# A Fourier transform and two gated networks on one core: weights loaded straight to their final tiles, sign as a product, a PSUM bank for constants alone, another order of loads

## Chip, core and metric

One of the eight cores of a Trainium2 chip runs the kernel. The metric is the device time of one execution in microseconds (us); of several runs the median counts.

The core has a matrix engine (TensorE, PE in the profile), three engines for elementwise work (VectorE or DVE, ScalarE or ACT, GpSimd or POOL), and SyncE (SP), which here only issues transfers (DMA). Each engine runs its own instructions in program order and waits on semaphores for the others. SBUF is the working memory; PSUM, with eight banks, takes the matmuls' results.

## The reference

```python
def _attn_ref(x):                      # x: (2, 3008, 256)
    X = np.fft.fft(x, axis=1)
    X = np.fft.fft(X, axis=2)
    return X.real.astype(np.float32)

def _moe_ref(x, w_gate, w_val, w_out): # 6016 tokens, 256 -> 1536 -> 256
    gate = 1.0 / (1.0 + np.exp(-(x @ w_gate)))
    val = x @ w_val
    return (gate * val @ w_out).astype(np.float32)

def _moe2_ref(x, w_in, w_out):         # 256 -> 2048 -> 256
    h = x @ w_in
    g = h * np.cos(h)
    return (g @ w_out).astype(np.float32)
# out = _moe2_ref(_moe_ref(_attn_ref(x).reshape(6016, 256), ...), ...)
```

x is float32; the weights arrive as 64-bit floating point numbers.

## The kernel before

**Stages.** Stage A multiplies x with a 47-point transform in 16 chunks of 8 products (a product of 32-bit floats is two instructions on TensorE, so 16 a chunk); ScalarE copies each chunk from PSUM into D1 (line 376). Chunk c uses the pair of PSUM banks `b0 = 2 * (c % 4)` and the next (line 356). x comes in eight pairs of chunks through three buffers `raws` (`load_x2`), each load issued by SP when the pair three before it has been read. Stage B (`stage_b`, "b00" to "b15", 12 groups) and stage C (`stage_c`, "c00" to "c12", 6 pieces) finish the transform; each copies its results out as a high part (ScalarE) and a low part (VectorE, line 443), since the matmuls behind work in a shorter format and take high and low part separately. Stage C writes into `eo[0]` to `eo[5]`.

**First network.** `step1(s)` runs for s = 0 to 71: six pieces of the tokens, each with 12 slices of 128 hidden units. A step has two halves `ab(s, 0)` and `ab(s, 1)` of six matmuls; VectorE combines them (`even`, `tokens`, lines 532 and 540); ScalarE takes the sigmoid (line 688), GpSimd multiplies (line 544). Four steps later 12 matmuls with the output weights follow (`out1`, lines 554 to 557). Steps 0 and 1 stand between the last pieces of stage C.

**Second network.** 192 steps of 12 matmuls, `hid` and `out2`. Its weights, decoded during the first network's steps, are kept in DRAM (`ws`) and loaded into the places of the first network's weights as these are done with (`w2_load`).

**Decoding a weight.** A unit holds 512 weights per partition. There are a small row ("row"), 12 units w1 (hidden), 6 units wo1 (output) and 16 units w2. A 64-bit weight is two words, `lo` and `hi`. `dec_steps` gives its steps, `(engine, planned us, what to issue)`: ScalarE takes the magnitude of `hi` (line 134) and the carry of `lo` (line 135), VectorE clamps (line 115) and shifts (line 119), GpSimd adds the carry (line 130), and VectorE puts the sign back (line 148); once the first network's steps have begun, VectorE masks the sign (line 141) and GpSimd adds it. A w1 unit then takes a sum and a difference (lines 171 and 172). `hilo_steps` splits the result into a high part (ScalarE, line 156) and a low part (GpSimd or VectorE, line 154). `clamp` and `shift` read two constants, `cmax` and `cmask`, from PSUM bank 7, columns 510 and 511.

**Where units lie.** Before the change a unit is loaded into a decode buffer of 1536 words per partition (line 164): first the six tiles `eo`, each until stage C needs it (`ENDS`), later four pieces `stages` of D1, two of them only until step 1 (`TWO`). The split writes the final tile `wr`; W1 and WO1 are views of it, W2 and WO2 too.

**Order of the work.** The order on each engine is made when the program is built, by a planner. It keeps a clock for each engine (`clk`) and a list of units under way (`live`). `slot(t, us, ahead)` is called before each group of matmuls: it issues the copies left by the group before (`after`), and then `fill(e, until)` puts onto each engine whatever decode steps end by its clock before `until`. `regular` and `spend` book the copies themselves. For SP, `fill` starts a new unit, and so its load, when a decode buffer is free and lasts long enough (`LIFE`). `need(key)` issues the rest of a unit at once when the program comes to its use. The matmuls' order is fixed; only their waits depend on the rest.

## Time and profile before

| | |
|---|---|
| runs, median (lowest to highest) | 1028.37 us (1027.06 to 1029.26) |
| the profiled execution | 1028.72 us |
| its span, first to last instruction | 1026.6 us |
| TensorE busy (its clock granted) | 999.1 us, 97% (0.991 of full) |
| VectorE, ScalarE, GpSimd busy | 763.2, 768.1, 684.2 us |
| moved by DMA | 85.59 MB |
| stage A | 4.1 to 44.8 us |
| stages B and C to the first step | 44.8 to 81.7 us |
| first network | 81.7 to about 500 us |

In rows of the timeline the numbers are start and busy time in us, the engine, the line, the operation, what it writes and reads, and in brackets the engine's idle time just before, with the instruction that ended it. Matmuls in a run are merged into one row with a count.

### The profile page before, as it was taken

To read this page: it belongs to the slowest core of one execution; us is meant where nothing else is said; L and a number is where in the kernel's file an instruction comes from. 1 tells how busy PE (TensorE), PEld (TensorE's weight loads), DVE (VectorE), ACT (ScalarE), POOL (GpSimd) and SP (SyncE) were. 2 spreads that over 40 slices of the span, in tenths; PEclk is the share of its full clock that TensorE was granted. 3 is DMA by queue.
4 is the path that set the end of the run, shared out by engine and by line. 5 is a ranking of instruction groups with operands and counts; after the bars stand their busy time and mean duration, and the time that the engine had idled before them with its cause. 6 is when DMAs were issued, how large, how long until landed. Compare 5 with 4: busy or idle time off the path is not lost.

```text
span 1026.6 us, 13189 instructions
## 1 busy us (share of the span) xinstructions
PE 999.1 (97%) x4566; PEld 833.5 (81%) x4566; DVE 763.2 (74%) x1037; ACT 768.1 (75%) x1212; POOL 684.2 (67%) x531
## 2 busy tenths in 40 slices
PE   7998988999999999999999999999999999999998
PEld 7986777888888888888788888888888888888886
DVE  4698985788787877776577777777777777777775
ACT  4666664767666675674788888888889888898886
POOL 2475985998989878885365665756557565665653
PEclk9899998999999999999999999999999999999999
DMA  8611754586776666788500000000000000000000
GB/s 280 227 53 41 152 117 91 113 177 162 162 163 144 160 155 142 177 218 215 130 1 21 1 21 21 0 21 1 21 19 3 21 1 21 0 21 21 1 21 21
DMA packets 25363, 85.59 MB, mean 83 GB/s; under 512 B 3248, under 2 KB 6640, under 8 KB 24624
## 3 DMA queue, kind: packets, MB, share of 16 engines
q0 software_dynamic: 10368, 37.02, 19.5%
q1 hardware_dynamic: 14672, 47.59, 13.4%
q8 instruction: 36, 0.59, 0.2%
q14 instruction: 31, 0.25, 0.1%
q10 hardware_dynamic: 256, 0.14, 0.1%
HBM read 33.16 MB, written 14.56 MB: 46 GB/s over the span
## 4 chain that ended last, share of the span: by engine, by line
PE 87%; DVE 4%; DMA 3%; ACT 2%; POOL 2%; issue 1%; SPq 0%; ACTq 0%; DVEq 0%; POOLq 0%
PE ps L596 25%; PE ps L514 14%; PE ps L515 14%; PE ps L516 14%; PE ps L554 6%; PE ps L557 6%; PE ps L556 6%; PE ps L363 1%; DVE D L540 1%; DMA raw<-in_x_dram 1%; DMA gh<-D 1%; POOL D L544 1%; DMA eo<-in_w_dram 1%; DVE eo L148 1%; PE ps L457 1%
## 5 line engine op out<-in xcount | busy, mean ns | idle before, releaser
L622 POOL TENSOR_TENSOR h<-D,h 128x502 fp32r<-128x502 f32 x191 | 284.5, 1490 | 216.2 <-ACT h L621 203.9
L596 PE MATMUL ps<-h,wr 128*128 128x502 f32 x1152 | 291.9, 389 | 0.0
L514 PE MATMUL ps<-es,wr 128*128 128x502 f32 x672 | 263.1, 391 | 3.9 <-DVE D L540 3.5
L515 PE MATMUL ps<-es,wr 128*128 128x502 f32 x672 | 262.4, 390 | 0.0
L516 PE MATMUL ps<-es,wr 128*128 128x502 f32 x672 | 261.4, 389 | 0.0
L596 PEld LDWEIGHTS ps<-h,wr 128*128 128x128 f32 x1152 | 217.6, 189 | 44.6
L544 POOL TENSOR_TENSOR D<-D 128x502 f32<-128x502 f32 x144 | 184.5, 1326 | 56.0 <-ACT D L688 55.2
L607 DVE SCALAR_TENSOR_TENSOR D<-D,ps 128x502 f32<-128x502 int32 x192 | 130.1, 678 | 118.6 <-POOL h L622 107.7
L540 DVE TENSOR_TENSOR D<-D,ps 128x1004 f32<-128x1004 f32 x144 | 172.9, 1201 | 49.1 <-PE ps L516 30.3
L688 ACT ACTIVATE D<-D 128x1004 f32<-128x1004 f32 x72 | 75.2, 1044 | 125.7 <-DVE D L540 125.6
L514 PEld LDWEIGHTS ps<-es,wr 128*128 128x128 f32 x672 | 126.7, 189 | 32.2 <-DVE D L540 4.8
L608 DVE SCALAR_TENSOR_TENSOR D<-D 128x502 f32<-128x502 int32 x192 | 144.8, 754 | 6.6
L606 ACT ACTIVATE D<-ps 128x502 int32<-128x502 f32 x192 | 113.0, 589 | 48.0 <-PE ps L516 46.0
L516 PEld LDWEIGHTS ps<-es,wr 128*128 128x128 f32 x672 | 126.7, 189 | 26.4
L515 PEld LDWEIGHTS ps<-es,wr 128*128 128x128 f32 x672 | 126.9, 189 | 25.6
L614 DVE TENSOR_TENSOR D<-D,ps 128x502 f32<-128x502 f32 x192 | 128.9, 671 | 16.1 <-ACT D L613 16.1
L532 DVE SCALAR_TENSOR_TENSOR D<-eo,w,ps 128x502 f32<-128x502 f32 x144 | 101.4, 735 | 38.1 <-PE ps L516 37.7
L612 ACT ACTIVATE D<-D 128x502 f32<-128x502 f32 x192 | 119.2, 621 | 12.2 <-DVE D L608 9.8
L613 ACT ACTIVATE D<-D 128x502 f32<-128x502 f32 x192 | 120.0, 625 | 6.1
L557 PE MATMUL ps<-gh,wr 128*128 128x502 f32 x288 | 113.2, 393 | 4.2 <-POOL wr L154 4.2
L556 PE MATMUL ps<-gh,wr 128*128 128x502 f32 x288 | 113.7, 395 | 1.2 <-ACT wr L156 1.2
L621 ACT CAST h<-D 128x502 fp32r<-128x502 f32 x192 | 114.7, 597 | 0.2 <-DVE D L614 0.2
(89 smaller groups left out, 1073.2 us busy)
## 6 DMA issues: line engine op xcount, KB each, us to landing
gh<-D POOLq DMA_DIRECT2D x72, 502.0 KB, 4.8
D<-in_w_dram SPq DMA_DIRECT2D x17, 512.0 KB, 5.1
ws<-D SPq DMA_DIRECT2D x16, 512.0 KB, 3.5
wr<-ws SPq DMA_DIRECT2D x16, 512.0 KB, 4.9
out_dram<-D SPq DMA_DIRECT2D x24, 251.0 KB, 3.2
eo<-in_w_dram SPq DMA_DIRECT2D x11, 512.0 KB, 6.2
raw<-in_x_dram SPq DMA_DIRECT2D x15, 256.0 KB, 4.7
D<-in_wo_dram SPq DMA_DIRECT2D x6, 512.0 KB, 4.2
```

The source lines that it names most:

```text
L514: PE.matmul(o, w_hi, m_hi, start=first, stop=False)
L515: PE.matmul(o, w_lo, m_hi, start=False, stop=False)
L516: PE.matmul(o, w_hi, m_lo, start=False, stop=last)
L540: V.tensor_tensor(out=gv[s][:, :, c:c + PC], in0=sas, in1=ps[:, 6:8, 0:PC], op=op)
L544: G.tensor_tensor(out=gv[p][:, 1, m], in0=gv[p][:, 1, m], in1=gv[p][:, 0, m], op=ALU.mult)
L556: PE.matmul(o, WO1[:, f, 0, m], h[:, 0, sl], start=(f == 0), stop=False)
L557: PE.matmul(o, WO1[:, f, 1, m], h[:, 0, sl], start=False, stop=False)
L596: PE.matmul(o, WO2[:, f, i, d * 128:(d + 1) * 128], h[:, m], start=(f == 0 and i == m == 0), stop=(f == NF2 - 1 and m == 1))
L607: V.scalar_tensor_tensor(out=r, in0=k, scalar=-C1, in1=h, op0=ALU.mult, op1=ALU.add)
L608: V.scalar_tensor_tensor(out=r, in0=k, scalar=-C2, in1=r, op0=ALU.mult, op1=ALU.add)
L614: V.tensor_tensor(out=r, in0=r, in1=ps[:, 4 + s % 4, 0:PC], op=ALU.mult)
L622: (V if s == N2S - 1 else G).tensor_tensor(out=h[:, 1], in0=r, in1=f32(h[:, 0]), op=ALU.subtract)
```

## The change

The first network's weights (w1 and wo1) are loaded into tiles of the size of a final weight tile (`slot_tile`, one tag for each place); the decode reads the raw words there, works in a decode buffer, and the split writes a new tile in the same place. Loads and decoding are thus planned apart: `load_next` issues the next of the 18 loads whenever SP's clock has room, and `begin` starts a unit's decode when its load is due and a buffer is free. W1, WO1, W2 and WO2 become functions that return a view of a slot. `stages` has two pieces in place of four, and the time limit TWO goes.

Units begun after group "b05" (`masked`) take the sign from ScalarE (Sign into one word of the pair, the magnitude into the other) and a product over each pair on VectorE. The other units put the sign back before GpSimd's add; the form with a masked sign and a second add on GpSimd goes.

Stage A rotates over three pairs of banks (0 to 5), the constants stay in bank 7, the warm-up products (seven for five) write bank 6. In the first loads x's second pair goes ahead of all weights, one weight stands between the second and the third pair, and up to chunk 2 SP plans less far ahead. Both memsets of x buffers are on GpSimd. Planned times of the groups change (1.71 to 1.79, 2.54 to 2.72), as do `ENDS` and `LIFE`.

The diff, cut to its core:

```diff
-NWARM = 5
+NWARM = 7
...
-    wr = cpool.tile([128, NF1 * 8 * 128 + NF1 * 2 * 256], F32R, name="wr")
...
+    slots, gen = {}, {}
+
+    def slot_tile(u, dtype):
+
+        gen[u] = gen.get(u, -1) + 1
+        slots[u] = cpool.tile([128, 2 * UC], dtype, tag=f"u{u}", name=f"u{u}_{gen[u]}", bufs=1)
+        return slots[u]
+
+    for u in range(NF1 + NF1 // 2):
+        slot_tile(u, F32)
+
+    def W1(f):
+        return slots[f].rearrange("p (g e h m) -> p g e h m", g=2, e=2, h=2)
...
-    stages = [flat1[:, i * 3 * UC:(i + 1) * 3 * UC] for i in range(4)]
+    stages = [flat1[:, i * 3 * UC:(i + 1) * 3 * UC] for i in range(2)]
...
-    czero = ps[:, 7, 509:510].bitcast(U32)
...
+        if masked[0]:
+            mag = r[:, :, 1]
+            return [
+                (A, .52, lambda: carry(t)),
+                (A, .52, lambda: A.activation(out=r[:, :, 0], in_=hi, func=AF.Sign)),
+                (A, .52, lambda: A.activation(out=mag, in_=hi, func=AF.Abs, scale=2.0 ** -80)),
+                (V, .6, lambda: clamp(mag)),
+                (V, .6, lambda: shift(mag.bitcast(U32))),
+                (G, 1.5, lambda: add(mag, t)),
+                (V, 1.05, lambda: V.tensor_reduce(out=t, in_=r, axis=mybir.AxisListType.X, op=ALU.mult)),
+            ]
+        low = buf[:, 0:n] if direct else lo
...
-        ] + ([
-            (V, .6, lambda: V.scalar_tensor_tensor(out=hi.bitcast(U32), in0=hi.bitcast(U32), scalar=0x80000000,
-                                                   in1=czero.to_broadcast(list(hi.shape)),
-                                                   op0=ALU.bitwise_and, op1=ALU.bitwise_or)),
-            (G, 1.23, lambda: added(lo)),
-            (G, 1.23, lambda: added(hi)),
-        ] if begun[0] else [
-            (G, 1.23, lambda: added(lo)),
             (V, .6, lambda: V.scalar_tensor_tensor(out=u, in0=hi.bitcast(U32), scalar=0x80000000, in1=u,
                                                    op0=ALU.bitwise_and, op1=ALU.bitwise_or)),
-        ])
...
+            (G, 1.23, lambda: add(t, low)),
+        ]
...
+    def load(kind, i, raw):
+        DQ.dma_start(out=raw.bitcast(U32), in_=sources[kind](i).bitcast(U32))
...
-        steps = [(DQ, 1.5 * n / UC, lambda: DQ.dma_start(out=buf[:, 0:2 * n].bitcast(U32), in_=src.bitcast(U32)))]
-        steps += dec_steps(buf, n)
+        if kind in DIRECT:
+            steps = dec_steps(buf, n, slots[home(kind, i)], True)
+        else:
+            raw = buf[:, 0:2 * n]
+            steps = [(DQ, 1.5 * n / UC, lambda: load(kind, i, raw))] + dec_steps(buf, n, raw, False)
...
+    DIRECT = ("w1", "wo1")
+    queued = [("w1", f) for f in range(NF1)] + [("wo1", u) for u in range(6)]
+    todo = [("row", 0)] + queued + [("w2", u) for u in range(16)]
+    loaded = {}
...
+    def load_next():
+        k = queued.pop(0)
+        load(*k, slots[home(*k)])
+        loaded[k] = spend(DQ, 1.5) + 2.3
...
+    def begin(until):
+
+        while todo and todo[0] in loaded:
+            for bf in free:
+                at = max(loaded[todo[0]], bf[2])
+                if at <= until and at + LIFE <= bf[1]:
+                    start(bf)
+                    break
+            else:
+                return
...
         while True:
+            begin(until)
...
+                if step[0] is VG and e is V and begun[0]:
+                    continue
...
+                if e is DQ and clk[e] + 1.5 <= until:
+                    if queued:
+                        load_next()
+                        continue
+                    if len(todo) > held[0] and todo[0][0] == "w2":
...
-    LIFE, ALWAYS = 16.0, 1e9
+    LIFE, ALWAYS = 14.0, 1e9
...
-    ENDS = (44, 52, 54, 62, 70, 70)
+    ENDS = (45.5, 52.5, 57, 65, 73, 73)
...
-        G.memset(raws[1], 0.0)
-        V.memset(raws[2], 0.0)
+        for r in raws[1:]:
+            G.memset(r, 0.0)
...
         for p in range(1, NX2):
-            fill(DQ, clk[DQ] + 2.0)
             load_x2(p)
+            if p == 1:
+                fill(DQ, clk[DQ] + 1.6)
...
-            PE.matmul(ps[:, 7, 0:128], warm, warm, start=True, stop=True)
+            PE.matmul(ps[:, 6, 0:128], warm, warm, start=True, stop=True)
...
-            slot(now, 1.71, AHA if c < NJC - 2 else (4, .4, 2, .5) if c < NJC - 1 else (4, .1, 2, -.8))
-            b0 = 2 * (c % 4)
+            slot(now, 1.79, (.3,) + AHA[1:] if c < 3 else AHA if c < NJC - 2 else (4, .4, 2, .5) if c < NJC - 1 else (4, .1, 2, -.8))
+            b0 = 2 * (c % 3)
...
         if st == "b05":
-            two_end[0] = now + 6 * 1.71 + 3 * 2.54 + 2.0
-            free += [[bf, ALWAYS, now] for bf in stages[:2]] + [[bf, TWO, now] for bf in stages[2:]]
+            masked[0] = True
+            free += [[bf, ALWAYS, now] for bf in stages]
...
     def w2_load(u):
-        nc.sync.dma_start(out=f32(wr[:, u * 2 * UC:(u + 1) * 2 * UC]), in_=ws[u])
+        nc.sync.dma_start(out=f32(slot_tile(u, F32R)), in_=ws[u])
```

## Rows read from the trace of the kernel before

**Rows 1.** Busy time by stage: stretch, length, engines, granted clock, DMA share, GB/s.

```profile
0.00:4.10 4.10, 2.26 (x10) 2.29 (x11) 2.48 (x6) 0.00 (x0) 2.15 (x6) 1.00 0.53 156
4.10:44.76 40.66, 34.94 (x261) 34.34 (x260) 20.37 (x37) 22.43 (x37) 10.71 (x10) 0.87 0.85 274
44.76:81.71 36.95, 33.33 (x241) 30.64 (x241) 35.15 (x63) 24.75 (x60) 27.25 (x22) 1.00 0.21 70
106.92:147.86 40.94, 40.94 (x181) 33.91 (x180) 34.96 (x40) 26.05 (x31) 36.37 (x32) 1.00 0.62 130
190.13:500.00 309.87, 308.17 (x1350) 254.29 (x1349) 237.51 (x267) 202.94 (x235) 257.44 (x225) 1.00 0.74 173
```

**Rows 2.** Timeline of TensorE in stage A.

```profile
5.30 3.06 PE L363 MATMUL ps<-hd,raw 128*128 128x96 f32 x26
11.20 7.20 PE L363 MATMUL ps<-hd,raw 128*128 128x96 f32 x48 [2.83 <-DMA raw<-in_x_dram]
...
21.27 2.89 PE L363 MATMUL ps<-hd,raw 128*128 128x96 f32 x24 [0.65 <-DMA raw<-in_x_dram]
26.41 18.35 PE L363 MATMUL ps<-hd,raw 128*128 128x96 f32 x136 [2.25 <-DVE eo L119]
```

**Rows 3.** Timeline of VectorE before TensorE's wait of 2.25 us ends.

```profile
25.67 0.69 DVE L119 SCALAR_TENSOR_TENSOR eo<-eo,ps 128x512 uint32<-128x512 uint32 x1
```

**Rows 4.** Single microseconds after the two gaps; the clock is the third number from the end.

```profile
13.00:14.00 1.00, 1.00 (x7) 1.00 (x6) 0.68 (x2) 1.00 (x4) 0.00 (x0) 0.50 0.68 209
...
29.00:30.00 1.00, 1.00 (x7) 1.00 (x7) 0.18 (x1) 0.79 (x2) 0.00 (x0) 0.50 0.79 123
```

**Rows 5.** Timeline of ScalarE: copies of stage A's chunks out of PSUM.

```profile
10.18 0.78 ACT L376 COPY D<-ps 128x768 f32<-128x768 f32 x1
...
13.29 0.79 ACT L376 COPY D<-ps 128x768 f32<-128x768 f32 x1
...
37.65 0.80 ACT L376 COPY D<-ps 128x768 f32<-128x768 f32 x1 [0.99 <-PE ps L363]
39.44 0.80 ACT L376 COPY D<-ps 128x768 f32<-128x768 f32 x1 [0.99 <-PE ps L363]
```

**Rows 6.** Timeline of TensorE at steps 12 to 16 of the first network.

```profile
147.86 0.40 PE L514 MATMUL ps<-es,wr 128*128 128x502 f32 x1
...
154.19 0.50 PE L557 MATMUL ps<-gh,wr 128*128 128x502 f32 x1 [2.36 <-POOL wr L154]
...
179.05 0.40 PE L514 MATMUL ps<-es,wr 128*128 128x502 f32 x1
```

**Rows 7.** Timeline of SP's DMA issues between 110 and 140 us.

```profile
122.12 1.46 SPq L164 DMA_DIRECT2D D<-in_wo_dram  x2
```

**Rows 8.** Busy time by stretch at the start; the last two numbers are DMA.

```profile
0.00:5.00 5.00, 3.16 (x15) 3.19 (x16) 2.88 (x7) 0.55 (x1) 2.15 (x6) 1.00 0.61 174
5.00:25.00 20.00, 15.69 (x121) 15.26 (x120) 8.40 (x20) 11.64 (x21) 2.81 (x3) 0.91 0.95 307
```

**Rows 9.** Timelines of ScalarE and TensorE where the first network begins.

```profile
87.17 0.67 ACT L134 ACTIVATE D<-D 128x512 f32<-128x512 f32 x1 [3.00 <-DMA D<-in_wo_dram]
...
91.28 0.49 PE L457 MATMUL ps<-D2h,T3h 128*128 128x502 f32 x1 [1.26 <-ACT eo L468]
```

**Rows 10.** Groups by line and shape: count, busy us and mean ns, idle before.

```profile
L540 DVE TENSOR_TENSOR D<-D,ps 128x1004 f32<-128x1004 f32 x144 | 172.9, 1201 | 49.1 <-PE ps L516 30.3 <-ACT gh L629 13.7 <-DMA gh<-D 1.0
...
L141 DVE SCALAR_TENSOR_TENSOR D<-D,ps 128x512 uint32<-128x512 uint32 x19 | 12.9, 681 | 0.0
L148 DVE SCALAR_TENSOR_TENSOR eo<-eo 128x512 uint32<-128x512 uint32 x11 | 11.4, 1038 | 4.8 <-POOL eo L130 4.8
...
L134 ACT ACTIVATE D<-D 128x512 f32<-128x512 f32 x23 | 15.4, 670 | 4.4 <-DMA D<-in_wo_dram 3.0 <-DMA D<-in_w_dram 1.4
```

**Rows 11.** Groups by line: ScalarE's table loads, first and last of three.

```profile
L134 ACT ACT_TABLE_LOAD x1 | 1.3, 1283 | 4.5 <-DVE raw L332 4.5
...
L613 ACT ACT_TABLE_LOAD x1 | 1.3, 1283 | 0.0
```

More of the change, by code (lines that the diff above doesn't have):

```diff
@@ L120, in shift, with dec_steps, carry, add @@
                                op0=ALU.logical_shift_left, op1=ALU.bitwise_and)
-    def dec_steps(buf, n):
+    def dec_steps(buf, n, raw, direct):
+        lo, hi = (raw.rearrange("p (n t) -> p n t", t=2)[:, :, k] for k in range(2))
         r = buf[:, 0:2 * n].rearrange("p (n t) -> p n t", t=2)
-        lo, hi = r[:, :, 0], r[:, :, 1]
         t = buf[:, 2 * n:3 * n]
         u = t.bitcast(U32)
-        def added(w):
-            G.tensor_tensor(out=t.bitcast(I32), in0=t.bitcast(I32), in1=w.bitcast(I32), op=ALU.add)
+        def carry(dst):
+            A.activation(out=dst.bitcast(I32), in_=lo.bitcast(U32), func=AF.Copy, scale=2.0 ** -29)
+        def add(dst, other):
+            G.tensor_tensor(out=dst.bitcast(I32), in0=dst.bitcast(I32), in1=other.bitcast(I32), op=ALU.add)
+        if masked[0]:
[10 more added lines that the diff above has]
+        low = buf[:, 0:n] if direct else lo
@@ new lines, in hilo_steps, with high, low @@
+    def hilo_steps(views, src):
+        at = []
+        def high():
+            at[:] = views()
+            A.copy(at[0], src)
+        def low(e):
+            e.tensor_tensor(out=at[1], in0=src, in1=f32(at[0]), op=ALU.subtract)
+        return [(A, .52, high), (VG, .6, low)]
+    ws = [dpool.tile([128, 2 * UC], F32, name=f"ws{u}") for u in range(NF2)]
+    sources = {"row": lambda i: w1s, "w1": lambda i: w1[i], "wo1": lambda i: wo1[i], "w2": lambda i: w2[i]}
+    def load(kind, i, raw):
+        DQ.dma_start(out=raw.bitcast(U32), in_=sources[kind](i).bitcast(U32))
@@ L195, in cost @@
     def cost(step, e):
-        return step[1] * (2.05 if step[0] is VG and e is G else 1) + (beside[0] if e is V else 0)
+        return step[1] * ((2.5 if begun[0] else 2.05) if step[0] is VG and e is G else 1) + (beside[0] if e is V else 0)
     def step_of(un, e=None):
@@ L290, in fft_moe_moe @@
     free += [[b_, e_, 0.0] for b_, e_ in zip(flat, ENDS)]
+    start(free[0])
     after = []
@@ L445, in stage_b @@
         after.append(evac)
-        return now + 1.71
+        return now + 1.79
     def stage_c(b, ch, ahead=AHB):
-        slot(now, 2.54, ahead)
+        slot(now, 2.72, ahead)
         t = b * NCH + ch
@@ L582, in hid @@
         for k in range(2):
-            three(o, W2[:, f, k, 0], W2[:, f, k, 1], y[:, 0, k], y[:, 1, k], first=(k == 0), last=(k == 1))
+            three(o, W2(f)[:, k, 0], W2(f)[:, k, 1], y[:, 0, k], y[:, 1, k], first=(k == 0), last=(k == 1))
     def out2(s):
@@ L681, in step1 @@
         if main:
-            for un in [un for un in live if un[1] and un[1][1] < (TWO if s < 2 else ALWAYS)]:
-                finish(un)
-            free[:] = [bf for bf in free if bf[1] == ALWAYS or bf[1] == TWO and s == 0]
+            free[:] = [bf for bf in free if bf[1] == ALWAYS]
             tokens(s)
```

103 lines of the change are left out of this document (48 added, 55 removed).

## Prediction

> **What bounds the kernel now.** The profiled execution took 1028.72 us, of which the span is 1026.6; it stands 0.35 us above the median of the three runs (1028.37). I read four views, coarse to fine. First the table by stage [rows 1]: from 190.13 to 500 TensorE is busy 308.17 of 309.87 us, and of the second network behind it the change touches only the tiles that hold its weights, so nothing is for sale there. Before that, stage A (to 44.76) has idle time and a mean granted clock of 0.87. So the question is only what happens before 190 us.
>
> Second, TensorE's own timeline in stage A, the 16 chunks of the first transform [rows 2]. Its idle pieces are 2.83 us (waiting for x), 0.65 (for x) and 2.25 (for a VectorE instruction that only decodes a weight). The 2.25 is odd until one counts: the run of 24 instructions before it is chunk 6 (16) and the first half of chunk 7 (8), so the instruction that waits is the first to write bank 7 of PSUM. The constants that `clamp` and `shift` read lie in that bank at columns 510 and 511, and the matmuls write columns 0 to 383 of it: the wait is on the bank, not on data. It ends when the `shift` that starts at 25.67 is done [rows 3]. After both long gaps the granted clock is half, 1.2 in place of 2.4 GHz [rows 4]. At full clock a chunk takes 1.79 us (copies of successive chunks at 37.65 and 39.44 [rows 5]), 0.1117 us an instruction. The 136 instructions after the bank wait took 18.35 us and would take 15.2; the 48 after the x wait took 7.20 and would take 5.4. Stage A thus loses 5.7 us idle and 5.0 us to the clock; TensorE alone would end it at 4.1 + 16 x 1.79 + 0.6 (the extra products of chunk 4) = 33.3.
>
> Third, the 36.95 us from 44.76 to 81.71, stages B and C up to the first network [rows 1]: VectorE is busy 35.15 us of it, TensorE 33.33. VectorE is the co-bound here, on decoding.
>
> Fourth, the steps of the first network. From 106.92 on TensorE is busy 40.94 of 40.94 us [rows 1], at 5.46 us a step (24 matmuls). Steps 12 and 16 start at 147.86 and 179.05 [rows 6]: 31.19 us for four steps that should take 21.84. The 9.35 us are two like waits for an output unit, the first of which ends at 154.19, and their low clock. Their cause is a load: the last two output units were requested only at 122.12 [rows 7], because a unit could be loaded only into a free decode buffer.
>
> **The change part by part.**
>
> *Own bank for the constants.* Stage A now rotates over three pairs of banks, 0 to 5, and the warm-up writes bank 6. The 2.25 us wait goes and with it the 3.15 us of low clock behind it. What comes late next is data.
>
> *Order of x and weights.* I followed the planner's clock for the load queue by hand (1.5 a weight, 2.1 a pair of chunks). Old: w0, x1, w1, x2, w2, x3, w3, x4, x5, w4, x6, tables, x7. New: x1, w0, x2, w1, x3, w2, w3, x4, w4, x5, w5, x6, tables, x7, then the other 12 units in a row. So x1 no longer queues behind 512 KB, which at 307 GB/s [rows 8] is 1.7 us; of the 2.83 us I leave 1. But in front of x7 there is now one weight more. x is 96 rows of 16 x 1024 numbers, 6.3 MB; with six weights, the tables and the head it is 10.1 MB. The first 5 us moved 0.87 MB and the next 20 ran at 307 GB/s with the DMA engines 0.95 busy [rows 8], so x7 lands near 5 + 9.2/0.307 = 35, and two chunks later stage A ends near 39, by transfers, not by TensorE. On SP each x load still waits for its buffer, and behind it wait only weights that are early. **Stage A: -5.8** (bounds: -11.5, TensorE alone; 0, the low-clock stretches come back).
>
> *Loads straight into the final tiles.* All 18 loads are issued by about 35 us and need no decode buffer; no byte moves that did not move before. The decode itself is the same until stage B's sixth group. The four staging buffers in D1 become two: a raw unit no longer sits in one while it loads. The 9.35 us at steps 12 to 16 go if those units are decoded by then; with their data there 80 us earlier, they are. **-9.3** (bounds -9.4 and 0). The load that ScalarE waits 3.00 us for at 87.17 also goes, and with it the 1.26 us that TensorE then waits for ScalarE's copy [rows 9]: **-1.3** (0 to -3).
>
> *What VectorE pays.* It was busy only 20.37 of 40.66 us in stage A [rows 1] because weights were late, and what it did not do then it does in B and C. New, by 39 us the six early units are decoded: six times some 3.1 (two at 0.68, a sign instruction at 1.04 [rows 10], half of the two sums), with its other work about 27 us. Up to 81.71 it did 58.0 in all (2.48 + 20.37 + 35.15 [rows 1]). If the four output units that it decoded after that come before it, at some 2.5 each, and the memset of 1.8 goes to POOL, it is 67, so 40 are left when stage A ends and the first step starts 40 us later; if they stay behind, 30 are left and TensorE's own 12 x 1.79 + 4 x 2.73 = 32.4 decide. The planner puts them ahead wherever its clock has room, and it charges 0.6 for instructions that take 0.68 to 1.04. I take 38.5 for these stages in place of 36.95: **+1.5** (bounds -4.5, +5.5).
>
> *Sign as a product.* Units begun after stage B's sixth group take ScalarE one instruction more (0.67), VectorE two at 0.68 and a reduction over 1024 numbers in place of three at 0.68 [rows 10], and POOL one add less. No row shows the reduction; the nearest is the addition over 1004, 1.20, which I take (bounds 0.68, the 512-element form, and 2.4, twice the addition). Some 20 units pay it, 16 of them second-network weights during the steps, at +0.5 us of VectorE each. In the steps VectorE is busy 237.51 of 309.87 us [rows 1], so 1.3 of each 5.46 are free beside today's decoding, and there is one unit in 3.6 steps: **0** (if that cover were gone, 16 x 0.5 = +8; POOL's relief cannot gain while TensorE is full). Two rows stand beside each other here: the instruction with two SBUF inputs, L148, takes 1038 ns, and the like one with an input from PSUM, L141, 681 [rows 10]. The Trainium skill, page SBUF — State Buffer, section "Who interferes with whom", says that a VectorE instruction with two SBUF inputs contends with GpSimd and that a reduction on this chip never does. The trace agrees on the first half; no run here shows the second, and by it the 1.20 would hold beside a busy POOL.
>
> *Edits at nothing.* The warm-up starts 0.9 us earlier, as it no longer waits for memsets in its bank, and is two products longer; the first real matmul still comes at 4.1. The planner's new lengths (1.71 to 1.79 and so on) only change order.
>
> Sum: 1028.7 - 5.8 + 1.5 - 1.3 - 9.3 = 1013.8; against the median, **1013.5 us**.
>
> **Rivals.**
> 1. *VectorE takes all of stage A's gain.* The first step starts no earlier than now. For it: 35.15 of 36.95 us busy. Against: its idle half of stage A is now filled. 1028.4 - 1.3 - 9.3 = 1017.8.
> 2. *TensorE alone bounds B and C*, and stage A ends at 36 with 0.9 to the next matmul as now: first step at 69.3, 12.4 earlier, 1005.
> 3. *The change does not do what it says at the steps:* the last output units are loaded early but decoded late, since only two decode buffers remain, and the stalls stay. For it: the decode of those units now takes from 122 to 154 us. 1013.5 + 9.3 = 1022.8.
> 4. *Slower: the copy out of PSUM becomes the wait.* ScalarE runs in order, and a chunk's copy stands behind the first decode instruction of a weight still in flight: the copies of chunks 0 and 1 came at 10.18 and 13.29 [rows 5], 3.7 and 4.9 us after their matmuls (done by 6.5 and 8.4 [rows 2]). With four pairs a copy may be 3 x 1.79 us late, with three 2 x 1.79 = 3.6: it decides from there. If each of six early weights makes TensorE wait 2.5 us and lose 2.5 to the clock (the means of the two cases above), stage A loses 30 us and ends at 63: 1013.5 + 24 = 1037.
> 5. *Sign needs another activation table.* Now there are three table loads of 1.28 us in the whole run, the first before Abs and the last before Sin [rows 11], and Abs and copies stand between sigmoids without one. Two more for each of 16 units would be 41 us of ScalarE; with half of it hidden in its idle third, 1013.5 + 20 = 1034. The Trainium skill, ScalarE: Activation LUTs, section "Table sets: the hidden batching unit", names relu, copy, identity and abs as being in every set, and not sign; by the 2.7 us that it gives for a switch, an estimate, the 41 would be 86. The trace agrees for Abs and copy and shows no Sign.
>
> **How the numbers follow.** Forecast 0.57 (its own range 1007 to 1020), rival 1 0.15, rival 2 0.10, rival 3 0.09, rival 4 0.05, rival 5 0.04. The range takes in 1 and 2 and leaves out 3 to 5: **1005 to 1021**. A difference of 0.2% (2 us) is about what a measurement of this kernel can tell from none. Faster: forecast and rivals 1 to 3, 0.91. Slower: rivals 4 and 5 but for a mild form of them, 0.07; within 0.2%: 0.02.
>
> **What would show it.** Right: no TensorE wait on a decode instruction in stage A, and its end at 38 to 40 us; the gap at 8 to 11 us down to about 1 and no half clock behind it; the first step at 76 to 80 us; steps from the fourth on at 5.46 us with no wait for output weights; still three table loads; the reduction at 1.2. Wrong: TensorE waiting for ScalarE's copies in stage A (rival 4), TensorE waiting for VectorE's low parts in B and C (rival 1), waits for output weights after step 8 (rival 3), table loads at each unit (rival 5).

## The result, and the profile after

The changed kernel took 1012.95 us (median of four runs, 1012.53 to 1017.06) beside 1028.82 us for the kernel before on the same chip: ratio 0.985, 95% interval 0.982 to 0.989. A second set of six runs gave 1015.03 beside 1026.85: 0.989 (0.987 to 0.992). So 12 to 16 us are gone. The forecast was 1013.5.

The profiled execution of the changed kernel has a span of 1011.5 us where that of before had 1026.6. Its table by stage answers [rows 1]; columns are a stretch in us, its length, busy time (instructions) of each engine, granted clock, share of the DMA engines and GB/s:

```profile
4.10:39.79 35.69, 32.40 (x262) 31.51 (x260) 18.74 (x33) 23.15 (x39) 17.30 (x18) 0.95 1.00 337
39.79:75.16 35.37, 33.33 (x240) 30.65 (x241) 29.92 (x56) 26.07 (x63) 32.61 (x30) 1.00 0.28 109
75.16:100.79 25.63, 20.56 (x87) 15.51 (x86) 20.94 (x25) 19.13 (x29) 14.82 (x13) 1.00 0.11 21
100.79:147.31 46.52, 46.52 (x205) 38.40 (x204) 40.62 (x45) 30.89 (x38) 40.80 (x36) 1.00 0.61 125
```

Stage A ends at 39.79 instead of 44.76, the first step starts at 75.16 instead of 81.71, and from the first output product in step 4 (100.79) TensorE is busy without a gap to 147.31, where before it waited at steps 12 and 14. In stages B and C VectorE is no longer full (29.92 of 35.37 us; before 35.15 of 36.95); GpSimd is now the busier of the two.

TensorE's timeline of stage A, which answers [rows 2]:

```profile
5.25 3.33 PE L427 MATMUL ps<-hd,raw 128*128 128x96 f32 x26
9.13 5.92 PE L427 MATMUL ps<-hd,raw 128*128 128x96 f32 x48 [0.56 <-issue]
...
17.59 14.37 PE L427 MATMUL ps<-hd,raw 128*128 128x96 f32 x112 [2.08 <-ACT D L440]
32.43 7.36 PE L427 MATMUL ps<-hd,raw 128*128 128x96 f32 x64 [0.48 <-DMA raw<-in_x_dram]
```

No wait on a decode instruction is left, and the 2.83 us wait for x is gone. In their place stands one wait of 2.08 us for ScalarE's copy out of PSUM, with low clock behind it (112 instructions take 14.37 us; at 0.1117 each they take 12.5). ScalarE's timeline tells why:

```profile
12.19 0.77 ACT L440 COPY D<-ps 128x768 f32<-128x768 f32 x1
16.18 0.66 ACT L161 ACTIVATE eo<-u 128x512 f32<-128x512 f32 x1 [3.22 <-DMA u<-in_w_dram]
16.75 0.78 ACT L440 COPY D<-ps 128x768 f32<-128x768 f32 x1
```

The copy that TensorE needs stands in ScalarE's queue behind the first decode instruction of a weight that was still in flight. That is rival 4 in a mild form. The seventh pair of x chunks, whose load ends the wait at 32.43, decides when the last four chunks begin.

At the start of the network one wait stayed, which answers [rows 9]:

```profile
85.21 0.49 PE L521 MATMUL ps<-D2h,T3h 128*128 128x502 f32 x1 [1.12 <-ACT eo L532]
```

The product that replaced the masked sign, and two of the three table loads; columns: line, engine, operation, count, then busy us and mean ns of one, then idle us before it:

```profile
L156 DVE TENSOR_REDUCE D<-D 128x512 f32<-128x1024 f32 x21 | 25.4, 1212 | 0.0
L750 ACT ACT_TABLE_LOAD x1 | 1.3, 1283 | 0.0
L677 ACT ACT_TABLE_LOAD x1 | 1.3, 1283 | 0.0
```

### The profile page after: what moved, and what is told of

The parts are those of the page before. It is cut to its first block, busy times and chain, and to the rows that moved or that the text cites. A ratio compares the mean times of both kernels' runs of the same rounds, so it can differ in the third digit from the quotient of the medians.

```text
span 1011.5 us, 13127 instructions
## 1 busy us (share of the span) xinstructions
PE 993.6 (98%) x4570; PEld 828.7 (82%) x4570; DVE 764.0 (76%) x1023; ACT 782.4 (77%) x1234; POOL 670.5 (66%) x525
## 4 chain that ended last, share of the span: by engine, by line
PE 85%; POOL 4%; DVE 3%; ACT 3%; DMA 3%; issue 1%; ACTq 0%; SPq 0%; DVEq 0%; POOLq 0%
PE ps L660 26%; PE ps L578 14%; PE ps L579 14%; PE ps L580 14%; PE ps L618 6%; PE ps L620 6%; PE ps L621 6%; DVE D L604 2%; POOL eo L145 1%; DMA u<-in_w_dram 1%; DMA gh<-D 1%; POOL u L179 1%; POOL eo L206 1%; ACT gh L693 1%; ACT gh L692 1%
## 5 line engine op out<-in xcount | busy, mean ns | idle before, releaser
L660 PE MATMUL ps<-h,u 128*128 128x502 f32 x1152 | 291.8, 389 | 0.0
L578 PE MATMUL ps<-es,u 128*128 128x502 f32 x672 | 262.9, 391 | 4.9 <-DVE D L604 3.5
L579 PE MATMUL ps<-es,u 128*128 128x502 f32 x672 | 262.2, 390 | 0.0
L580 PE MATMUL ps<-es,u 128*128 128x502 f32 x672 | 261.2, 389 | 0.0
L660 PEld LDWEIGHTS ps<-h,u 128*128 128x128 f32 x1152 | 217.4, 189 | 44.7
L578 PEld LDWEIGHTS ps<-es,u 128*128 128x128 f32 x672 | 126.4, 188 | 33.6 <-DVE D L604 4.7
L580 PEld LDWEIGHTS ps<-es,u 128*128 128x128 f32 x672 | 126.5, 188 | 26.5
L579 PEld LDWEIGHTS ps<-es,u 128*128 128x128 f32 x672 | 126.6, 188 | 25.6
L620 PE MATMUL ps<-gh,u 128*128 128x502 f32 x288 | 112.5, 391 | 0.0
L621 PE MATMUL ps<-gh,u 128*128 128x502 f32 x288 | 111.8, 388 | 0.0
```

Source lines behind the costliest of these rows:

```text
L578: PE.matmul(o, w_hi, m_hi, start=first, stop=False)
L579: PE.matmul(o, w_lo, m_hi, start=False, stop=False)
L580: PE.matmul(o, w_hi, m_lo, start=False, stop=last)
L620: PE.matmul(o, WO1(f)[:, 0, m], h[:, 0, sl], start=(f == 0), stop=False)
L621: PE.matmul(o, WO1(f)[:, 1, m], h[:, 0, sl], start=False, stop=False)
L660: PE.matmul(o, WO2(f)[:, i, d * 128:(d + 1) * 128], h[:, m], start=(f == 0 and i == m == 0), stop=(f == NF2 - 1 and m == 1))
```

## The experiments

Each kernel was profiled once, and all times in this table are read from TensorE's timeline: the end of the last matmul on x (end of stage A), the first matmul of the first network, the first output matmul (step 4), the time from there to the end (rest), and the span. `before_need1` has the program of before up to step 4, and the kernels marked * have that of the changed kernel in stage A.

| kernel | A ends | to first step | to step 4 | rest | span | DMA 5 to 35 us |
|---|---|---|---|---|---|---|
| before | 44.76 | 36.95 | 25.2 | 919.7 | 1026.6 | 264 GB/s |
| before_need1 | 43.27 | 37.51 | 25.0 | 912.0 | 1017.8 | 276 |
| before_bank | 41.04 | 35.87 | 25.5 | 919.8 | 1022.2 | 304 |
| before_two | 39.78 | 36.47 | 25.2 | 912.4 | 1013.9 | 315 |
| after * | 39.79 | 35.37 | 25.6 | 910.7 | 1011.5 | 326 |
| after_again * | 42.25 | 34.68 | 25.4 | 910.9 | 1013.3 | 320 |
| after_late_wo * | 44.19 | 34.75 | 25.4 | 911.0 | 1015.3 | 306 |
| after_sigmoid_later * | 40.35 | 34.86 | 25.6 | 910.6 | 1011.5 | 320 |
| after_no_eo * | 40.65 | 34.75 | 25.3 | 913.9 | 1014.6 | 312 |
| after_two_early * | 42.89 | 34.73 | 24.5 | 922.6 | 1024.7 | 310 |
| after_sign_old | 41.74 | 36.89 | 24.6 | 910.6 | 1013.9 | 306 |
| after_copyfirst | 41.95 | 36.35 | 25.1 | 911.1 | 1014.5 | 326 |
| after_bank4 | 48.95 | 34.39 | 25.6 | 910.5 | 1019.5 | 263 |
| after_x_sooner | 40.71 | 36.52 | 27.2 | 943.8 | 1048.3 | 289 |

### The bank alone

```diff
-            b0 = 2 * (c % 4)
+            b0 = 2 * (c % 3)
...
-            PE.matmul(ps[:, 7, 0:128], warm, warm, start=True, stop=True)
+            PE.matmul(ps[:, 6, 0:128], warm, warm, start=True, stop=True)
...
```

The lines left out move the extra products of chunk 4 to that chunk's own banks, as in the changed kernel.

> The kernel before with the bank edit alone: the chunks of stage A rotate over three pairs of PSUM banks and the warm-up writes bank 6; loads, order and decoding stay as they were. Own-bank theory: the 2.25 us wait and the 3.15 us of low clock behind it go, so stage A ends at 44.76 - 5.4 = 39.4 instead of 44.76, and the waits for output weights at steps 12 and 16 stay (9.35 us). Rival, transfers: the same x chunks come no sooner and stage A still ends after 43. For the stages behind it: if VectorE (35.15 us busy of 36.95) takes the gain back, the first step still starts at 81 to 82 and the total is 1028; if it does not, the first step starts at 76.3 and the total is 1023.

Measured: 0.9966 of before (0.9949 to 0.9983), 1023.45 us beside 1026.04. TensorE's timeline of stage A in this kernel:

```profile
11.33 7.20 PE L363 MATMUL ps<-hd,raw 128*128 128x96 f32 x48 [2.98 <-DMA raw<-in_x_dram]
...
21.07 10.93 PE L363 MATMUL ps<-hd,raw 128*128 128x96 f32 x96 [0.31 <-ACT half L386]
33.68 7.36 PE L363 MATMUL ps<-hd,raw 128*128 128x96 f32 x64 [1.68 <-DMA raw<-in_x_dram]
```

The wait on the decode instruction is gone, the long run behind it goes at full clock (96 in 10.93 us), and a wait for x of 1.68 us appears late in the stage: transfers take back part of the 5.4. Stage A ends at 41.04. The first step follows at 76.91, 4.8 us earlier than in the profile of before (3.9 earlier than in before_need1, which is the same program up to there), so VectorE does not take the gain. That was rival 1, and it is out for the stages as they were before, too. Of what the profile shows, 2.6 us are left in the median of the runs.

### The bank undone in the changed kernel

```diff
-            b0 = 2 * (c % 3)
+            b0 = 2 * (c % 4)
```

> The changed kernel with four pairs of PSUM banks in stage A again, so that the constants share bank 7 with every fourth chunk; everything else as changed. Own-bank theory: TensorE waits again for a decode instruction of VectorE (line 127 or 131) before a write of bank 7, 1 to 3 us at one or two chunks, with low clock behind it: stage A ends at 41 to 45 instead of 39.79. Rival, copy order: the third pair is what costs, because the copy of chunk 2 is late by more than two chunks and less than three; then the 2.08 us wait for ScalarE's copy goes, with its 1.9 us of low clock, and stage A ends at 36 to 38.

Measured: 1020.31 us, 0.9941 of before. Stage A:

```profile
17.68 5.43 PE L427 MATMUL ps<-hd,raw 128*128 128x96 f32 x24 [5.70 <-DVE eo L127]
23.66 11.78 PE L427 MATMUL ps<-hd,raw 128*128 128x96 f32 x104
```

Two waits on VectorE's decode instructions come back, 5.70 us here and 2.20 us (for line 131) at 37.64, and stage A ends at 48.95, 9.2 us later than in the first profile of the changed kernel, 7.3 later than the mean of six (below) and 4.2 later than before. The wait on the bank is shown from both sides, and in the new order of loads it would have cost more than in the old one: 5.3 us beside 1015.03 in the median of the runs, where the bank alone gave 2.6.

### Copies ahead of weights in flight

```diff
-        loaded[k] = spend(DQ, 1.5) + 2.3
+        loaded[k] = spend(DQ, 1.5) + (6.3 if k[0] == 'w1' and k[1] < 4 else 2.3)
```

> The changed kernel, in which the planner expects the first four weights 4 us later than it does now, so that ScalarE's first decode instruction of a weight in flight stands behind two copies out of PSUM instead of ahead of them. The load queue's order is the same. Copy-order theory: the 2.08 us wait of TensorE for a copy goes, and the 1.9 us that the 112 instructions behind it lost to the clock: stage A ends at 36 instead of 39.79, and the total falls by 2 to 4 us unless decoding takes it back in the next two stages. Rival, transfers bound stage A (as predicted, near 39): the wait only moves to x, stage A ends at 39 to 40, the total moves by less than 0.5 us.

Measured: 1014.7 us, 0.9882 of before (0.9851 to 0.9913), no different from the changed kernel. Stage A:

```profile
18.82 3.78 PE L427 MATMUL ps<-hd,raw 128*128 128x96 f32 x32 [1.75 <-DMA raw<-in_x_dram]
23.48 7.55 PE L427 MATMUL ps<-hd,raw 128*128 128x96 f32 x64 [0.88 <-DMA raw<-in_x_dram]
32.97 8.98 PE L427 MATMUL ps<-hd,raw 128*128 128x96 f32 x64 [1.94 <-DMA raw<-in_x_dram]
```

The wait for the copy is gone, and x takes its place three times. So the 2.08 us of the changed kernel lay under the wait for x. The load that ends the last of these waits was issued at 22.63, 2.2 us sooner than in the changed kernel (24.84), since its buffer was free sooner, and was there no sooner (32.97 beside 32.43): that speaks for the transfers and against the three buffers of x as what holds the stage.

### The last output units loaded late

```diff
-                    if queued:
+                    if len(queued) > (0 if released[0] else 2):
...
+        if s == 8:
+            released[0] = True
+            for u in (16, 17):
+                A.copy(slots[u][:, 0:1], halfpi)
```

The line that defines `released` is left out.

> The changed kernel, in which the last two output units' loads wait for a tiny ScalarE copy into their tiles at step 8 (about 120 us), when in the kernel before they were requested too; their tiles, the direct load and all other edits stay. Load theory (the early load is what removed the stalls): ScalarE begins to decode the first of them at 128 or later instead of 123.3, TensorE waits for its weights at step 12 and perhaps at step 16 with low clock behind each, and the total rises by 5 to 9 us. Rival, decode order: the units are decoded one after the other in two buffers anyway, the load at 120 us is early enough, and the total stays within 1 us of 1013.

Measured: 1014.76 us, 0.9884 of before (0.9854 to 0.9915). ScalarE's and, in the second fence, GpSimd's timeline:

```profile
124.36 0.27 ACT L714 COPY u<-halfpi 128x1 f32<-128x1 f32 x2
...
128.63 0.67 ACT L142 ACTIVATE D<-u 128x512 int32<-128x512 uint32 x1 [2.13 <-DMA u<-in_wo_dram]
```

```profile
145.25 1.79 POOL L179 TENSOR_TENSOR u<-D,u 128x512 fp32r<-128x512 f32 x1
```

The loads were let go only at 124.5, relative to the first step even later than before (45.6 us after it; before 122.12 - 81.71 = 40.4 [rows 7]). Decoding began at 128.63, as the load theory says. But no wait for output weights came back: the rest took 911.0 us as in the changed kernel. The unit for step 12 was ready at 147.0, and that step's first output matmuls start at 149.08: two microseconds to spare. A late load, as before had it, is not enough to make the stalls.

### Decoding placed one step earlier in the kernel before

```diff
-            need(("wo1", (s - L1) // 2))
+            need(("wo1", min(5, (s + 1 - L1) // 2)))
```

> The kernel before with one edit: the decoding of an output unit has to be issued one step earlier than the step that uses it (the planner's forced finish looks one step ahead). Loads, buffers, banks and the sign's form stay as before, and the last two output units are still requested at about 122 us. Placement theory (the stalls at steps 12 and 16 came from where the planner put the decoding, not from the load): both waits go or shrink under 0.5 us and the total falls by 7 to 9 us, to about 1018. Load theory, as predicted: the data is late, the 2.36 us waits stay, and the total stays within 2 us of before.

Measured: 1018.6 us, 0.9924 of before (0.990 to 0.9947): 8.2 us less from one line that moves no load. The rest fell from 919.7 to 912.0. SP's timeline from 110 to 140 us and, in the second fence, the one wait for output weights that TensorE's timeline still shows:

```profile
120.99 1.46 SPq L164 DMA_DIRECT2D D<-in_wo_dram  x2
```

```profile
129.72 0.49 PE L557 MATMUL ps<-gh,wr 128*128 128x502 f32 x1 [1.70 <-DVE wr L154]
```

The last two units are requested 40.2 us after the first step, where before it was 40.4 [rows 7], and the pairs of waits at steps 12 and 14 are gone. This refutes the sentence of the prediction "Their cause is a load". The wait of 1.70 us is more than the 0.5 expected: the forced finish put a low part on VectorE, and that instruction took 4.88 us (from 124.78), while GpSimd was busy.

### One output unit's place undone in the changed kernel

```diff
-    ENDS = (45.5, 52.5, 57, 65, 73, 73)
+    ENDS = (45.5, 52.5, 57, 65, 66, 66)
```

> The changed kernel with one constant changed: the last two output tiles close as decode buffers at 66 instead of 73 on the planner's clock, so that two output units instead of three are decoded before the first steps of the network. All 18 loads stay where they are, done by about 45 us, straight into the final tiles. Placement theory: the third unit slips behind steps 1 to 4, in which the planner has no room on VectorE, every later unit slips with it, and TensorE waits for output weights again at step 12 or 14, 1 to 4 us a time with low clock behind it: the total rises by 5 to 10 us, to 1019 to 1025. Load theory, as predicted: with the data in place 80 us early the units are in time, and the total stays within 1.5 us of 1014.

Measured: 1024.39 us, 0.9985 of before (0.9974 to 0.9996): nearly all of the change is lost. TensorE's timeline at steps 8 and 12:

```profile
124.68 0.49 PE L620 MATMUL ps<-gh,u 128*128 128x502 f32 x1 [0.58 <-ACT u L176]
126.98 0.50 PE L621 MATMUL ps<-gh,u 128*128 128x502 f32 x1 [1.80 <-POOL u L179]
151.01 0.50 PE L620 MATMUL ps<-gh,u 128*128 128x502 f32 x1 [0.57 <-ACT u L176]
153.32 0.49 PE L621 MATMUL ps<-gh,u 128*128 128x502 f32 x1 [1.81 <-POOL u L179]
```

These are pairs like those of before at steps 12 and 14, of which [rows 6] shows one wait, though all 18 loads were issued by 42.2 us. GpSimd's timeline shows where the six units became ready. In this kernel:

```profile
77.74 1.30 POOL L179 TENSOR_TENSOR u<-D,u 128x512 fp32r<-128x512 f32 x1 [3.13 <-ACT u L176]
...
109.14 1.84 POOL L179 TENSOR_TENSOR u<-D,u 128x512 fp32r<-128x512 f32 x1
...
125.40 1.53 POOL L179 TENSOR_TENSOR u<-D,u 128x512 fp32r<-128x512 f32 x1
134.60 1.60 POOL L179 TENSOR_TENSOR u<-D,u 128x512 fp32r<-128x512 f32 x1
151.73 1.54 POOL L179 TENSOR_TENSOR u<-D,u 128x512 fp32r<-128x512 f32 x1
160.33 1.59 POOL L179 TENSOR_TENSOR u<-D,u 128x512 fp32r<-128x512 f32 x1
```

and in the changed kernel:

```profile
75.75 1.29 POOL L179 TENSOR_TENSOR u<-D,u 128x512 fp32r<-128x512 f32 x1 [0.63 <-ACT u L176]
78.88 1.30 POOL L179 TENSOR_TENSOR u<-D,u 128x512 fp32r<-128x512 f32 x1 [1.83 <-ACT u L176]
...
84.76 1.28 POOL L179 TENSOR_TENSOR u<-eo,u 128x512 fp32r<-128x512 f32 x1 [3.31 <-ACT u L176]
...
118.85 1.57 POOL L179 TENSOR_TENSOR u<-D,u 128x512 fp32r<-128x512 f32 x1
...
124.21 1.57 POOL L179 TENSOR_TENSOR u<-D,u 128x512 fp32r<-128x512 f32 x1
...
140.60 1.58 POOL L179 TENSOR_TENSOR u<-D,u 128x512 fp32r<-128x512 f32 x1
```

The changed kernel finishes three output units before the network runs at full pace; this one finishes one and has the second at 109 (I had expected two). Before had two, ready at 84.6 and 94.6. From 84.0 to 103.5 in the changed kernel (89.4 to 109.5 before), which is steps 1 to 4, VectorE decodes nothing, so in this planner's order each unit that misses the start pushes the later ones behind it, and each needs several steps of leftover time. The unit for step 12 comes at 125.8 in the changed kernel, at 153.3 here, and came at 154.1 before [rows 6].

### Two small edits to the kernel before

```diff
-            need(("wo1", (s - L1) // 2))
+            need(("wo1", min(5, (s + 1 - L1) // 2)))
...
-            b0 = 2 * (c % 4)
+            b0 = 2 * (c % 3)
```

> The kernel before with two small edits together: the own bank for the constants (three pairs of banks, warm-up in bank 6) and the decoding of an output unit issued one step earlier. Loads still go through decode buffers in their old order, the sign has its old form. Theory after the runs so far: the bank gave 0.0034 and the placement 0.0076 of the time of before, and nothing else of the change carries time; so these two edits give 0.989 of before, some 1015.4 us, as the changed kernel (0.985 to 0.989). Rival: direct loads and their order carry a part of their own in stage A and B (as predicted, about 3 us): these two edits stop at 1018 or more.

Measured: 1016.53 us, 0.9909 of before (0.9891 to 0.9926). The intervals of the changed kernel are 0.9823 to 0.9886 and 0.9871 to 0.9915, of which only the second meets it. So two small edits carry most of the change, 10.4 of its 11.8 to 15.9 us; the changed kernel's two medians lie 1.5 and 3.6 us lower still, and that may belong to the rest of the change. Part of it is visible: the forced placement leaves one wait at a step,

```profile
125.42 0.50 PE L557 MATMUL ps<-gh,wr 128*128 128x502 f32 x1 [1.72 <-DVE wr L154]
```

and the rest takes 912.4 us here, 910.7 in the changed kernel. VectorE's timeline shows the instruction that TensorE waits for and, in the second fence, a like instruction in the kernel before, where GpSimd was idle beside it:

```profile
120.47 4.90 DVE L154 TENSOR_TENSOR wr<-D,wr 128x512 fp32r<-128x512 f32 x1
```

```profile
29.82 0.69 DVE L154 TENSOR_TENSOR wr<-eo,wr 128x512 fp32r<-128x512 f32 x1 [3.46 <-ACT wr L156]
```

### The old form of the sign

```diff
-                (A, .52, lambda: A.activation(out=r[:, :, 0], in_=hi, func=AF.Sign)),
...
+                (V, .6, lambda: V.scalar_tensor_tensor(out=hi.bitcast(U32), in0=hi.bitcast(U32), scalar=0x80000000,
...
-                (V, 1.05, lambda: V.tensor_reduce(out=t, in_=r, axis=mybir.AxisListType.X, op=ALU.mult)),
+                (G, 1.23, lambda: add(t, hi)),
...
```

> The changed kernel with the old form of the sign for the units that use the product: VectorE masks the sign bits, POOL makes two additions, no Sign on ScalarE and no reduction. Prediction: worth 0, so the total moves by less than 1 us. A rival that came out of the late loads: the stalls at steps 12 and 16 went because the decoding of an output unit became shorter or was placed earlier, not because of its load; if it is the sign's form that did it, TensorE waits 1 to 3 us for the last two output units' low parts again, and the total rises by 5 to 9 us.

Measured: 1015.11 us beside 1015.03 for the changed kernel on the same chip (0.9881 and 0.9893 of before): 0, as predicted, and no stall came back. The windows from 147.31 to 500, the old form in the first fence and the changed kernel in the second (PE, PEld, DVE, ACT, POOL):

```profile
147.31:500.00 352.69, 350.71 (x1539) 289.76 (x1538) 267.83 (x303) 232.18 (x275) 282.18 (x246) 1.00 0.68 160
```

```profile
147.31:500.00 352.69, 350.83 (x1537) 289.35 (x1536) 275.46 (x304) 244.51 (x293) 261.02 (x228) 1.00 0.69 159
```

VectorE pays 7.6 us more for the product and GpSimd 21 less; TensorE is full either way. In the one profile of the old form stages B and C took 36.89 us, 2 more than in the changed kernel, with VectorE busy 34.93 of them, and the way to step 4 was 0.9 shorter; the medians of the runs show nothing of it.

### The changed kernel once more

> The changed kernel itself once more, as the control for the others on the same chip. In the look at the late output loads, stage A, whose instructions were the same, ended at 44.2 instead of 39.79, with the DMA engines moving 306 GB/s from 5 to 35 us instead of 326. If stage A is bound by transfers (as predicted), its end follows that rate from run to run: some 39.8 at 326 GB/s and 44 at 306; at a like rate the span is 1011 to 1012. If the copy order decides, it ends at 39 to 40 whatever the rate.

Measured: 1015.03 us, as above; in the profile stage A ended at 42.25 with 320 GB/s, span 1013.3. TensorE's timeline from the first copy wait on:

```profile
17.33 14.37 PE L427 MATMUL ps<-hd,raw 128*128 128x96 f32 x112 [1.54 <-ACT D L440]
33.26 8.98 PE L427 MATMUL ps<-hd,raw 128*128 128x96 f32 x64 [1.56 <-DMA raw<-in_x_dram]
```

The rate is only part of it: after_sigmoid_later ended at 40.35 with the same 320. Over six profiles of the same instructions (the kernels marked *) the end of stage A ran from 39.79 to 44.19, mean 41.7. Profiles that differ by 2 us in stage A thus tell nothing, and the 39.79 of the first one was the best of six.

### The first sigmoid behind the copies, and no weight in the output tiles

These two go together. First:

```diff
+        if s == 1:
+            A.activation(out=gv[0][:, 0], in_=gv[0][:, 0], func=AF.Sigmoid)
...
-            A.activation(out=gv[s][:, 0], in_=gv[s][:, 0], func=AF.Sigmoid)
+            if s:
+                A.activation(out=gv[s][:, 0], in_=gv[s][:, 0], func=AF.Sigmoid)
```

> The changed kernel with the first sigmoid put behind the copies of the second batch's second slice (line 532) on ScalarE, not ahead of them. Theory: TensorE's 1.12 us wait at 85.2 is for copies that stand behind that sigmoid, which itself waits for the tokens; it goes, and the total falls by 1 to 1.5 us unless the gate of step 0 now comes late. Rival: the gate of step 0 is what the next steps need, and POOL's products start later by as much: the total stays or rises by up to 1 us.

Measured: 1014.03 us (0.9885 of before), and the wait stands as it was, 1.13 us at 85.26. The theory is wrong as stated; ScalarE's timeline shows another instruction ahead of the copies:

```profile
84.11 0.62 ACT L176 CAST u<-eo 128x512 fp32r<-128x512 f32 x1 [4.11 <-DVE eo L156]
84.64 1.05 ACT L532 COPY eo<-ps 128x502 f32<-128x502 f32 x2
```

A weight was being decoded in the very tile that the copy writes, so its last instructions had to go first. The second attempt took that weight out of the tile:

```diff
-    ENDS = (45.5, 52.5, 57, 65, 73, 73)
+    ENDS = (45.5, 52.5, 57, 65, 66, 66)
...
-            need(("wo1", (s - L1) // 2))
+            need(("wo1", min(5, (s + 1 - L1) // 2)))
```

> The changed kernel in which no weight is decoded any more in the last two output tiles shortly before they are written (their closing times in the planner go from 73 to 66), and the decoding of an output unit is issued one step earlier to keep its margin. Theory: TensorE's 1.12 us wait at 85.2 is for copies (line 532) that stand behind the last instruction of a weight decoded in their target tile, which itself waits for a reduction of VectorE behind the tokens of step 0; the wait goes and the total falls by about 1 us. Rival: the unit that has to move then comes late at the steps, TensorE waits 1 to 3 us there, and the total rises.

Measured: 1015.86 us (0.9906 of before). The wait stays, 1.59 us at 85.16, and now it is the sigmoid that is ahead:

```profile
83.60 1.04 ACT L750 ACTIVATE D<-D 128x1004 f32<-128x1004 f32 x1 [2.21 <-DVE D L604]
84.55 1.52 ACT L532 COPY eo<-ps 128x502 f32<-128x502 f32 x3
```

Both were in front, and taking one away uncovered the other. Both edits together were not tried.

This kernel also bears on the output units. It differs from after_two_early in the `need` line alone, and like it has one output unit ready before the network runs at full pace (77.7 us, the second at 109.6). Its rest is 913.9 us, where after_two_early has 922.6 (medians of the runs 1015.86 and 1024.39), and none of the pairs of waits is left.

### Fewer weights ahead of x

```diff
-            slot(now, 1.79, (.3,) + AHA[1:] if c < 3 else AHA if c < NJC - 2 else
+            slot(now, 1.79, (.3,) + AHA[1:] if c < 3 else (2 if c < 5 else -9,) + AHA[1:] if c < 10 else AHA if c < NJC - 2 else
```

(with the edit of after_copyfirst)

> The changed kernel with two weights fewer (1 MB) ahead of the last two pairs of x chunks on the load queue, and with the first four weights expected 4 us later so that ScalarE's copies go first. Transfer theory: at 320 GB/s the last pair lands 3.3 us sooner and stage A ends at 37 to 39 instead of 39.8 to 42.2; the weights come later by as much, and if the decoding in the next two stages takes all of that back, the first step still starts at 75 to 77; if not, at 72 to 74 and the total falls by 2 to 3 us. Rival: copies out of PSUM or buffers of x decide, stage A stays at 40 or more.

Measured: 1049.02 us, 1.0222 of before (1.0202 to 1.0241). Stage A ended at 40.71, not at the 37 to 39 of the transfer theory but inside the spread of the six profiles, so it decides nothing between theory and rival. The loss is at the steps:

```profile
120.11 0.79 PE L620 MATMUL ps<-gh,u 128*128 128x502 f32 x1 [4.46 <-ACT u L176]
121.47 0.79 PE L621 MATMUL ps<-gh,u 128*128 128x502 f32 x1 [0.56 <-POOL u L179]
134.62 0.49 PE L620 MATMUL ps<-gh,u 128*128 128x502 f32 x1 [0.57 <-ACT u L176]
136.93 0.50 PE L621 MATMUL ps<-gh,u 128*128 128x502 f32 x1 [1.82 <-POOL u L179]
```

Such pairs stand at five steps, down to 187.97, and the rest took 943.8 us. The fifth and sixth weights were issued from 30.99 us on, where the changed kernel issues them at 14.75 and 22.10. The decoding of the output units slid behind the start of the network, and 33 us were lost, with every load issued by 44 us. The edit of after_copyfirst alone lost nothing (rest 911.1).

## Why the prediction was right, and where it was not

The time was right (1013.5 for 1012.95 and 1015.03), but in part by luck: of the four terms of the sum the one for stage A was more than twice too large, the largest had the right size for a wrong reason, and the two small ones had the wrong sign.

**Own bank for the constants: right.** The wait is on the bank, shown by doing it alone and by undoing it. Of the 5.4 us that the prediction counted for the wait and its low clock, 2.2 to 5.0 came in stage A (before 44.76 and 43.27; with the bank 41.04 and 39.78) and 2.6 in the time of the runs.

**Order of x and weights, and stage A as a whole: mis-sized.** The term was -5.8, to 39. Two profiles of the old program give 44.0, six of the new one 41.7: -2.3. Before with the bank alone ended at 41.04, with bank and placement, which has the same stage A, at 39.78. So the new order of the loads shows no gain of its own. That x comes last, by its transfers, was right: x waits took the place of the copy wait when that was removed, and a load issued 2.2 us sooner landed no sooner (after_copyfirst). (That the DMA engines are busy 1.00 of the stage shows less, since 12 more weights follow x.) The rate was not too high either: 306 to 326 GB/s came where the sum had 307. What the sum left out are TensorE's waits under the transfers. It let the stage end two chunks behind the last pair of x, at full clock. In four of the six profiles TensorE waits for the pair before that one, until 32.43 to 35.21 us, so that four chunks are still to come, and in three of the four these take 8.98 us instead of 7.15, at the low clock that the prediction gave only as a bound.

**Loads straight into the final tiles: right size (-9.3 forecast, -8.9 measured), wrong step.** The prediction read at 122.12 that the units were requested late [rows 7] and at 154.19 that they were late [rows 6], and made the first the cause of the second. Requested later still, they were in time (after_late_wo); requested 80 us early, they were late (after_two_early); without moving a load, 8 us were won (before_need1). What decides is where the decoding stands in the engines' order. In the changed kernel it came sooner because three output units instead of two are decoded before step 1, and VectorE decodes nothing from then to step 4. That number is one way to move the place and not the only one: with two units (before_need1) or one (after_no_eo) decoded early, and each later one forced a step sooner, the rest is 912.0 and 913.9 us and no pair of waits is left. The step that failed is "if those units are decoded by then; with their data there 80 us earlier, they are", and before it "Their cause is a load". Rival 3 named the very condition, loaded early but decoded late, and gave it 0.09; after_two_early and after_x_sooner are that rival. Which of the edits brought the third unit in (the free buffers, `LIFE`, `ENDS`, the planned times) was not told apart; that `ENDS` alone can put it out again was shown. (All 18 loads were issued by 40.9 us, not by about 35.)

**What VectorE pays: wrong sign** (+1.5 forecast; 34.7 to 35.4 us in four profiles of the same program up to there, for 36.95 and 37.51, so -2.3). The step that failed is that VectorE's work sets the length of these stages: it was busy 29.92 us where the sum had 38.5, and GpSimd went from 27.25 to 32.61. The lines show what moved: of 14 sums and differences of w1 units in these stages VectorE made 9 before and 2 after (6.7 and 1.4 us), GpSimd 5 and 12 (4.4 and 10.4 us). That this shift is what shortened the stages was not tested. (The sum's 67 is 66.2 by its own terms, 58.0 and four times 2.5 less 1.8, which changes nothing here.) Rival 1 is out. Rival 2 is out by its stage A, which ended at 39.79 to 44.19 for its 36; the 33.3 us that it gave to B and C, by TensorE alone, are nearer to the measured 34.7 to 35.4 than the forecast's 38.5.

**ScalarE's wait for a load at the start: wrong** (-1.3 forecast; to step 4 it took 25.2 before, 25.4 to 25.6 in three profiles of the changed kernel). The load wait went, but TensorE's wait is for copies that have two other things ahead of them in ScalarE's queue.

**Sign as a product: right.** Forecast 0 with +0.5 us of VectorE a unit and a reduction of 1.20; measured 0, +7.6 for some 16 units, and 1.212. The Trainium skill, page SBUF — State Buffer, section "Who interferes with whom", has it that a reduction does not contend with GpSimd here, and the trace agrees: all 22 reductions took 1209 to 1215 ns, 1209 the one at 73.76 us with GpSimd busy throughout, 1214 the one at 136.27 with GpSimd idle.

**Rival 4** came in the mild form that the chances allowed for, in the first profile at one chunk in place of six, 2.08 us and 1.9 of low clock; removing it won nothing, as x was next. **Rival 5** is out: the table loads are three, as before.

Summed over the profiles: -2.3 in stage A, -2.3 to the first step, +0.3 to step 4 and -8.9 after it make -13.2, where the forecast had -5.8, +1.5, -1.3 and -9.3, which is -14.9. The sum came near because it had 3.5 us too much gain in stage A and 3.8 too little on the way to the first step, which is luck.

## What to carry to other kernels

When something is requested late and is late, delay the request in one kernel and advance it in another before calling it the cause: here both left the outcome as it was, and the place of the work in the planner's order decided. Where a stage's leftover time is short, count the pieces that must be done before it begins; each one missing can push all behind it, and here two weights held back by 9 to 16 us upstream cost 33. And when an in-order engine holds up another, look at everything that stands ahead in its queue, for taking one away may only show the next.

## What the runs showed of the hardware

The same instructions in stage A, with the DMA engines full, moved 306 to 326 GB/s from 5 to 35 us from one execution to the next, and ended the stage between 39.79 and 44.19 us. Sign on ScalarE, 22 times before and between the sigmoids, brought no table load: the three of 1283 ns are all there are. The subtraction of a unit's high part on VectorE, with both inputs in SBUF, took 0.69 us beside an idle GpSimd (before, at 29.82) and 4.88 and 4.90 us beside a busy one (before_need1 at 124.78, before_two at 120.47); the reduction, with one input, took 1.21 us either way. And the clock did not answer to the length of a gap alone: after 1.54 us idle 112 matmuls took 14.37 us instead of 12.5 (after_again), after 1.75 us 32 took 3.78 where 3.6 is full clock (after_copyfirst).
